# Two halves of one kernel, sliding-window attention and an SSM convolution, put into one schedule with shared memory phases

## The chip, the cores and the metric

The kernel runs on one core of a Trainium2 chip. The metric is the device time of one execution in microseconds (us). Every kernel was run with the kernel before beside it on the same chip, and medians are quoted. Names used below: PE is the matmul engine, PEld its weight load, DVE the vector engine, ACT the scalar engine, POOL the fourth compute engine, SP the engine whose queue issues most DMAs. A "kgen end" is the moment at which ACT begins to write the last part of one chunk's convolution kernel; that write takes another 0.4 us, or 1.6 us in the old form.

## The reference, cut to what matters

The output is the concatenation of two independent results, each 2048 x 640.

```python
def _A_ref(x, wqkv, wo):                       # attention: 32 heads of 20, window of 8 keys, 2 apart
    qkv = (x @ wqkv) ...                       # q, k, v: [1, 32, 2048, 20]
    idx = pos[:, None] - off[None, :]          # off = 0, 2, ..., 14
    logits = einsum("bhsd,bhswd->bhsw", q, k[idx]) * scale      # masked where idx < 0
    o = einsum("bhsw,bhswd->bhsd", softmax(logits), v[idx])
    return o @ wo

def _B_ref(u, A, B, C, log_dt, Dskip):         # SSM: a causal convolution of length 2048 per channel
    K = einsum("dn,dnl,dn->dl", Cc, exp(dt * A * l), dt * Bc).real      # 640 channels, 192 states
    y = irfft(rfft(pad(u)) * rfft(pad(K)))     # the FFT is done by matmuls in the kernel
    return y + u * Dskip
return concatenate([a, b], axis=-1)
```

There is no data that goes from one half to the other. What they share is the engines, SBUF (the on-chip buffer), the eight PSUM banks (where matmuls accumulate) and the DMA queues.

## The kernel before

The SSM half runs first, then attention, each with all eight PSUM banks and its own buffers. The SSM works on five chunks of 128 channels:

```python
for c in range(NCH):                       # NCH = 5; partB, with cuts
    X, Y = tables(tc, pools, c, Gd)        # DVE: powers of the states, from generators in DRAM (Gd)
    f1(..., U ..., A1, 0)                  # PE + ACT: first FFT stage of the input
    kgen(tc, pools, X, Y, Kd)              # PE: 512 small matmuls read X and Y; ACT evicts into Kd
    ...                                    # last chunk: load HB, the inverse FFT's table
    spread(tc, pools, C, Kd, K)            # PE + ACT
    f1(..., K ..., A1, 1)
    f2_prod(tc, pools, C, A1, Yf)          # PE + ACT + DVE: second stage and the product
    ia(tc, pools, C, Yf, Z)                # PE + ACT: first inverse stage
    nc.sync.dma_start(out=Zd[c][:], in_=Z[:])
...
Zall <- Zd                                 # DMA back, on two queues
for q in range(4):                         # inverse: 128 matmuls ps_ib, casts into ysb, DVE adds, store
    ...
```

X and Y have one buffer each, so `tables(c+1)` can't start before `kgen(c)` has read them. The generators are made in eleven rounds over all five chunks at once, ahead of the loop. The eviction in kgen writes with a stride:

```python
    for nt in (11, 11, 10):
        ps = pools["psum"].tile([128, nt, NB], f32, name="ps_k", tag="bank")     # eight banks
        ...
        nc.scalar.copy(out=Kd[:, :, t0:t0 + nt].rearrange("p b t -> p t b"), in_=ps[:])
```

Attention then does its projections, the products q*k on DVE ("prod") summed by matmuls, a softmax with maximum and sum on DVE, the products attn*v on DVE, summed by matmuls with the identity, and an output projection that contracts 32 rows at a time:

```python
    for d in range(DH):                    # 20 x 4 x 2 matmuls for 128 positions of each quarter, K = 32
        for sc in range(4):
            for eh in range(2):
                MM(pst[sc][eh][:], lhsT=o2[32*sc:32*sc+32, d, 128*q:128*q+128],
                   rhs=wo2[32*sc:32*sc+32, d, 320*eh:320*eh+320], ..., tile_position=(32*sc, 0))
```

## Time and profile before

| | kernel before |
|---|---|
| time | 666.22 us, median of 3 (662.37 to 669.65) |
| span of the profiled run | 664.6 us |
| SSM half | 0 to about 445 us |
| attention half | about 445 to 664.6 us |

The page of the profiled run gives each engine's busy time with its share of the span, and the busy tenths of 40 equal slices (16.6 us each):

```profile
PE 379.7 (57%) x6301; PEld 282.3 (42%) x6308; DVE 397.4 (60%) x578; ACT 261.1 (39%) x427; POOL 41.9 (6%) x43
...
PE   3400004775375457636761676415989944989895
...
DVE  1789647289539935991799205123009689876830
```

No engine is full over the span, but each slice has a different one that is nearly so: DVE in the prologue and in waves in the loop, PE in the projections (slices 29 to 32), DVE again in attention's products. From slice 23 to slice 30, the tail of the SSM and the start of attention, DVE does little.

The view of windows cuts the span by stage. Columns: stretch, length, then busy us (and count) of PE, PEld, DVE, ACT and POOL, then the granted PE clock, the DMA engines' mean busy share, and GB/s. The cuts are the ends of kgen(2) and kgen(4), and the end of the SSM.

```profile
0.00:251.50 251.50, 101.49 (x2368) 87.77 (x2369) 165.05 (x298) 102.51 (x139) 32.32 (x28) 0.86 0.33 89
251.50:382.80 131.30, 73.97 (x1704) 65.79 (x1705) 93.44 (x184) 56.86 (x95) 8.68 (x6) 0.71 0.11 33
382.80:445.00 62.20, 33.66 (x436) 30.48 (x435) 15.14 (x28) 31.31 (x61) 0.41 (x2) 0.77 0.59 205
445.00:664.60 219.60, 170.61 (x1793) 98.29 (x1800) 123.77 (x68) 70.45 (x133) 0.50 (x7) 0.86 0.20 54
```

Two periods of the chunk loop take 131.3 us, of which DVE works 93.4. The rest, about 19 us a period, is mostly the hole in which kgen reads the tables. DVE's timeline shows that hole (start, length, what ran; in brackets the idle time ahead of it and what ended it):

```profile
318.10 0.26 DVE L218 TENSOR_TENSOR Xtab<-Xtab,Xg 128x192 bf16<-128x192 bf16 x1 [15.80 <-DMA Xtab<-Gdram]
```

Groups of instructions that the change touches (total busy us, mean ns of one, then the engine's idle time ahead of them):

```profile
L516 DVE TENSOR_TENSOR prod<-qT,kT 128x5120 bf16<-128x5120 bf16 x16 | 44.2, 2820 | 35.9 <-ACT qT L494 33.8
L284 ACT CAST Kd<-ps_k 128x363 bf16<-128x363 f32 (+1 forms) x15 | 25.6, 1706 | 98.8 <-PE ps_k L282 98.8
...
L564 PE MATMUL ps_op<-wo_6012,o_6142 32*128 32x320 bf16 x640 | 42.9, 337 | 1.8 <-ACT ob L569 1.7
```

And one wait, of the inverse FFT on Z's way through DRAM (total us, times, longest):

```profile
PE ps_ib L427 <- DMA Zall<-Zdram_69: 9.6, 1, 9.6
```

### The profile page before, as it was taken

Reading aid. Unit: us, or ns where it says so; the run is one execution under the profiler, and the core shown is the slowest. Engines: PE = TensorE matmul, PEld = TensorE weight load, DVE = VectorE, ACT = ScalarE, POOL = GpSimd, SP = SyncE. Lnnn points to the kernel's source line nnn. Section 1 sums busy time; section 2 is a strip of 40 time slices with the busy share of each in tenths; the row PEclk is TensorE's granted clock in tenths of the full one; section 3 lists DMA queues with packets and bytes.
Section 4 is the critical chain, followed back from the end, with each engine's and each line's share of the span. In section 5 each row is a group of like instructions: output and inputs, shape, how many; then the busy total and the mean of one; then the engine's idle time right before and its main releaser. Section 6 shows DMA issues by size and latency. Waiting matters only on the chain. (4 is left out here: it accounts for less than half of the span.)

```text
span 664.6 us, 14150 instructions
## 1 busy us (share of the span) xinstructions
PE 379.7 (57%) x6301; PEld 282.3 (42%) x6308; DVE 397.4 (60%) x578; ACT 261.1 (39%) x427; POOL 41.9 (6%) x43
## 2 busy tenths in 40 slices
PE   3400004775375457636761676415989944989895
PEld 2200004665365446536551566414437622337355
DVE  1789647289539935991799205123009689876830
ACT  2865003375137524452553257333544431122222
POOL 2331200200020002000200000000000000000000
PEclk9999999986569757775876678667999975887997
DMA  3057992201110111011201093379700000001101
GB/s 91 31 152 234 262 230 54 44 1 65 37 44 1 65 38 43 1 64 39 43 1 64 3 369 140 139 162 317 175 0 3 5 0 1 0 1 41 40 15 66
DMA packets 44492, 51.27 MB, mean 77 GB/s; under 512 B 26384, under 2 KB 40976, under 8 KB 42256
## 3 DMA queue, kind: packets, MB, share of 16 engines
q1 hardware_dynamic: 33216, 33.48, 16.6%
q10 hardware_dynamic: 10512, 14.27, 7.4%
q0 software_dynamic: 704, 2.62, 2.0%
q8 instruction: 49, 0.80, 0.5%
q14 instruction: 11, 0.09, 0.0%
HBM read 33.44 MB, written 16.88 MB: 76 GB/s over the span
## 5 line engine op out<-in xcount | busy, mean ns | idle before, releaser
L277 PE MATMUL ps_k<-Ytab,Xtab 128*32 128x33 bf16 x1280 | 32.3, 278 | 67.8 <-DVE Xtab L220 35.5
L516 DVE TENSOR_TENSOR prod<-qT,kT 128x5120 bf16<-128x5120 bf16 x16 | 44.2, 2820 | 35.9 <-ACT qT L494 33.8
L284 ACT CAST Kd<-ps_k 128x363 bf16<-128x363 f32 (+1 forms) x15 | 25.6, 1706 | 98.8 <-PE ps_k L282 98.8
L218 DVE TENSOR_TENSOR Xtab<-Xtab,Xg 128x384 bf16<-128x384 bf16 (+2 forms) x35 | 14.8, 422 | 77.3 <-DMA Xtab<-Gdram 62.4
L277 PEld LDWEIGHTS <-Xtab 128*32 128x32 bf16 x1280 | 29.2, 184 | 70.6 <-issue 65.8
L357 PE MATMUL ps_ia<-cEA,Yf 128*32 128x256 bf16 x640 | 33.7, 395 | 27.3 <-DVE Yf L341 22.7
L314 PE MATMUL ps_f_521<-cBD_426,Uall 128*64 128x256 bf16 x4 | 0.7, 448 | 80.6 <-DVE Xtab L220 80.6
L314 PEld LDWEIGHTS <-Uall 128*64 128x64 bf16 x160 | 11.1, 205 | 81.6 <-issue 81.4
L564 PE MATMUL ps_op<-wo_6012,o_6142 32*128 32x320 bf16 x640 | 42.9, 337 | 1.8 <-ACT ob L569 1.7
L357 PEld LDWEIGHTS <-Yf 128*32 128x32 bf16 x640 | 30.3, 182 | 30.2 <-DVE Yf L341 23.6
L303 PE MATMUL ps_s<-Kd,cSEL 128*128 128x256 bf16 (+1 forms) x260 | 34.5, 307 | 8.4 <-ACT Kd L284 8.4
L564 PEld LDWEIGHTS <-o_6142 32*128 32x128 bf16 x640 | 31.3, 101 | 15.9 <-issue 12.7
L358 ACT CAST Z<-ps_ia 128x512 bf16<-128x512 f32 x40 | 23.7, 645 | 31.3 <-PE ps_ia L357 30.5
L237 POOL MEMSET Xtab<- 128x4608 bf16 x5 | 19.7, 3937 | 230.9 <-PE ps_k L282 230.6
L303 PEld LDWEIGHTS <-cSEL 128*128 128x128 bf16 x260 | 27.5, 115 | 14.7 <-issue 8.3
L339 DVE TENSOR_TENSOR Yf<-S 128x512 bf16<-128x512 bf16 x20 | 8.4, 420 | 34.5 <-ACT S L335 34.5
L519 PE MATMUL ps_l<-prod,Gs 128*32 128x256 bf16 x320 | 15.9, 343 | 21.8 <-DVE prod L516 21.8
L552 PEld LDWEIGHTS <-ident 128*128 128x128 bf16 x160 | 15.0, 102 | 30.6 <-issue 16.4
L282 PE MATMUL ps_k<-Ytab,Xtab 64*32 64x33 bf16 x1280 | 24.9, 239 | 5.3 <-issue 5.3
L555 ACT CAST o_6142<-ps_o 128x512 bf16<-128x512 f32 x20 | 10.2, 606 | 43.5 <-PE ps_o L552 43.5
L282 PEld LDWEIGHTS <-Xtab 64*32 64x32 bf16 x1280 | 21.6, 149 | 7.7 <-issue 6.4
L199 ACT ACTIVATE cs<-ph 128x1920 bf16<-128x1920 int32 x11 | 19.7, 1801 | 9.5 <-DVE ph L197 9.4
(725 smaller groups left out, 1010.8 us busy)
## 6 DMA issues: line engine op xcount, KB each, us to landing
Gdram<-cs SPq DMA_DIRECT2D x12, 480.0 KB, 3.1
HB<-k_HB SPq DMA_DIRECT2D x4, 1024.0 KB, 11.3
cT<-k_T ACTq DMA_DIRECT2D x1, 3072.0 KB, 24.1
Ytab<-Gdram SPq DMA_DIRECT2D x30, 96.0 KB, 2.7
Xg<-Gdram SPq DMA_DIRECT2D x5, 576.0 KB, 3.9
Uall<-in_B_u_dram POOLq DMA_DIRECT2D x4, 640.0 KB, 28.5
cSEL<-k_SEL ACTq DMA_DIRECT2D x1, 1664.0 KB, 9.7
wsb<-in_A_wqkv_dram SPq DMA_DIRECT2D x2, 800.0 KB, 21.9
```

The lines of the kernel that those rows point to most:

```text
L199: nc.scalar.activation(out=cst[:].rearrange("p c r n -> p r c n"), in_=ph[:].rearrange("p r (c n) -> p r c n", c=NCH), func=ACT.Sin, scale ...
L237: nc.gpsimd.memset(X[:, :, 20:NXS, :], 0.0)
L277: MM(o, lhsT=X[:, part, :, col], rhs=Y[:, part, :, col], start=(i == 0 and part == 0), stop=False, tile_position=(0, 32 * g), skip_group_c ...
L282: MM(o, lhsT=X[hb:hb + 64, part - 2, :, col], rhs=Y[hb:hb + 64, part - 2, :, col], start=False, stop=(part == 3), tile_position=(hb, 32 * ...
L284: nc.scalar.copy(out=Kd[:, :, t0:t0 + nt].rearrange("p b t -> p t b"), in_=ps[:])
L303: nc.tensor.matmul(o, lhsT=C["SEL"][:, wi, :], rhs=r, start=(j2 == 0 and n_ == 0), stop=(n_ == len(ops) - 1), skip_group_check=True)
L357: MM(o, lhsT=Yf[:, :, r, 4 * j + g], rhs=C["EA"][:, r, :], start=(jj == 0 and r == 0), stop=(r == 1), skip_group_check=True, tile_position ...
L358: nc.scalar.copy(out=Z[:, :, :, 4 * jq:4 * jq + 4].rearrange("p l r (j d) -> p (l r) j d", d=2), in_=ps[:].rearrange("p j l r d -> p (l r) ...
L516: V.tensor_tensor(out=pr[:], in0=q4[:, :, :, 256 * hf:256 * hf + 256], in1=k4[:, :, :, 256 * hf:256 * hf + 256], op=A.mult)
L519: MM(lps[w // 2][32 * sc:32 * sc + 32, w % 2, :], lhsT=Gs[:, ct, :], rhs=pr[:, ct, sc, :], start=(ct == 0 and w % 2 == 0), stop=(ct == 4), ...
L552: MM(ops[b][:].rearrange("p a b -> p (a b)"), lhsT=ident[:], rhs=p2[:, 2 * b:2 * b + 2, :].rearrange("p a b -> p (a b)"), start=(w == 0), ...
L564: MM(pst[sc][eh][:], lhsT=o2[32 * sc:32 * sc + 32, d, 128 * q:128 * q + 128], rhs=wo2[32 * sc:32 * sc + 32, d, 320 * eh:320 * eh + 320], s ...
```

## The change

The intent is to use one half's idle engines for the other half. The halves become one schedule. Projections, logits and softmax go under the SSM's prologue, attn*v goes into the chunk loop, and the output projection goes behind the inverse FFT with K=128, after a DMA that gathers heads across partitions. For that, memory is shared: buffers of one phase take the place of another's, and the eight PSUM banks are split by role (tags "l" 2, "a" 2, "b" 3, "k" 1). Work is cut on the way: no maximum in the softmax, its sum by matmuls, no zero slots in X, contiguous writes of Kd. The instruction order on each engine is set by a scheduler from the program's dependences, so the place of a call in the text is only a priority.

```diff
     for nt in (11, 11, 10):
-        ps = pools["psum"].tile([128, nt, NB], f32, name="ps_k", tag="bank")
+        ps = pools["psum"].tile([128, nt, NB], f32, name="ps_k", tag="k", bufs=1)
         ...
-        nc.scalar.copy(out=Kd[:, :, t0:t0 + nt].rearrange("p b t -> p t b"), in_=ps[:])
+        nc.scalar.copy(out=Kd[:, :, t0:t0 + nt], in_=ps[:].rearrange("p t b -> p b t"))
 ... (main)
-    partB(tc, pools, prm, B_u, B_Dskip, out_b)
-    partA(tc, pools, A_x, A_wqkv, A_wo, out_a, ident)
+    gens(tc, pools, ta, wi, Gd, 0, 1)          # generators of chunk 0 alone
+    make(0)                                    # tables(0), kgen(0)
+    a.transpose()
+    a.proj_qk(0)
+    a.logits(0)
+    gens(tc, pools, ta, wi, Gd, 1, 3)
+    a.proj_qk(1)
+    a.proj_v()
+    a.logits(1)
+    gens(tc, pools, ta, wi, Gd, 3, 5)
+    ... (release prologue buffers, load SEL and T)
+    avs = [(hf, dp) for hf in (1, 0) for dp in range(10)]
+    for c in range(NCH):
+        f1(U); spread; f1(K); f2_prod; ia      # arguments cut
+        nc.sync.dma_start(out=Zd[c][:], in_=Z[:])
+        if c + 1 < NCH:
+            make(c + 1)
+        ... (c == 3: release the tables, load HB in their place)
+        for hf, dp in avs[4 * c:4 * c + 4]:
+            a.av(hf, dp)
+    fp.release()                               # the FFT's buffers
+    ... Zall <- Zd, 5 DMAs, all on SP's queue
+    a.out_load()
+    a.gather(1)                                # 16 DMAs v2 -> oT
+    ... (inverse, as before, stores on SP's queue)
+    a.out_proj(1)
+    a.gather(0)
+    a.out_proj(0)
+    def av(self, hf, dp):                      # one of 20: two of the 20 head dimensions, 256 positions, 8 keys
+        p2 = self.pools["p2"].tile([128, W, 2, 256], bf16, name="p2", tag="p2")      # one buffer
+        V.tensor_tensor(out=p2[:], in0=windows(self.v2...), in1=self.at[hf]..., op=A.mult)
+        ps = self.psp.tile([128, 2, 256], f32, name="ps_o", tag="l", bufs=2)
+        for w in range(W):
+            nc.tensor.matmul(ps[:], lhsT=self.ident[:], rhs=p2[:, w], start=(w == 0), stop=(w == W - 1))
+        nc.scalar.copy(out=self.v2[:, d, HALO + 256 * hf:...], in_=ps[:])
+    def out_proj(self, hf):
+        ... 5 matmuls K=128 for each [128, 320], 160 in all, instead of 640 with K=32
```

## The prediction

> **What bounds the kernel now.** Two halves in series: in the table of windows SSM ends near 445 us, attention takes the last 220. No engine is full (page: PE 57%, DVE 60%, ACT 39%).
>
> - Prologue: in 20-66 us DVE is busy 40 of 46 us, PE 3.5.
> - Chunk loop: four periods of about 66.5 us (133-397), DVE 47-49, PE 38, ACT 30. In the timeline DVE builds tables(c+1) and f2's products in about 47 us, then idles 16 (301.9 to 318.1) while kgen reads the single table buffer.
> - SSM tail: spread, f1, f2, ia of the last chunk 383-415, Z to DRAM and back 9 us, inverse 424-445.
> - Attention: 15 us of x loading, 40 of projections, then DVE products and softmax (36.6 of 40 us in 525-565), output projection on PE.
>
> **What the change does.**
>
> DVE loses both max/sum reductions (14.8 us), subtract (4.6), half of x^T's casts (6.6): from 397 to about 370. Products keep their elements (44 each for logits and attn*v). Gens split into 1+2+2 chunks: 33 shorter rounds instead of 11, about +5 us on DVE and ACT, with one ph buffer.
>
> PE: the output projection goes from 640 K=32 matmuls (53 ns apart in the chain, 34 us) to 160 K=128, about 22 us (estimate: 320 columns at 216 ns per 512, the projections' pace).
>
> ACT: Kd's eviction now writes contiguously; it takes 1.7 us for 363 elements where other casts take 0.6 for 512: -15 us. Added: all x^T casts and about eight table loads of 1.28 us (Exp/Sin alternate). The Trainium skill, "ScalarE activation tables: per-element evaluation and per-set limits", section "What a function is on this engine", gives the same 1283 ns.
>
> Moved: projections, logits, softmax go under the prologue, tables(0) and tables(1); attn*v goes into the loop; 4 MB of Zall loads move from under the last chunk to behind it, as they reuse FFT buffers and follow Z(4) on one queue.
>
> **Sum, by DVE order** (build listing, trace durations):
> - Prologue: products 43, tables 66, gens 37, the rest 19 = 165 us, plus start and waits for projections: gens end near 200.
> - SEL and T load (11 and 26 us in before), f2(0) waits: loop proper from about 236.
> - Periods now carry attn*v: about 71, 79, 69 us to kgen(4)'s end, near 458. DVE stays the limit; kgen's wait of 15 us is only partly filled (two attn*v of 2.2 us), and kgen's single PSUM bank adds 2.
> - Tail: chain 31 us, Zall 18 (5 MB at about 300 GB/s; was 9), inverse 21, rest of output projection 20, gather and last store 5.
>
> Predicted **552 us**, range 512 to 598. Faster by over 2%: 0.96; within 2%: 0.03; slower: 0.01.
>
> **What would show it.** PE busy with attention in the first 200 us; DVE total 365-375 us, over 65% of the span; first loop chunk held by cT's DMA; DVE idle 10-14 us at kgen(2), (3), (4); PE idle 15-20 us before the inverse, ended by Zall's DMA; Kd casts below 0.8 us; output projection near 22 us of PE, after the inverse.
>
> **What would make it wrong.** In-order engines: a product ahead of table work holds DVE until ACT has evacuated q and k; two PSUM banks per role may starve PE. PE's clock (0.68-0.75 granted in the loop) may fall as PE gets denser. Gens' stores may block behind x loads on the SP queue. The other way: attn*v fills kgen's wait: 510.

## The result, and the profile after

| | before | after |
|---|---|---|
| median (range), 4 runs each on one chip | 667.17 us (662.37 to 669.65) | 584.19 us (583.37 to 585.86) |
| span of the profiled run | 664.6 us | 581.5 us |
| granted PE clock over the span | 0.821 | 0.839 |

The ratio is 0.8767, with a 95% interval of 0.8713 to 0.8822. A ratio is the mean time of one kernel's fast runs over that of the other's of the same rounds, so it isn't quite the ratio of the medians quoted. The change is worth 83 us, and 32 us less than predicted.

The page after, same lines (slices of 14.5 us):

```profile
PE 389.3 (67%) x5764; PEld 278.0 (48%) x5784; DVE 371.4 (64%) x646; ACT 268.1 (46%) x510; POOL 45.3 (8%) x60
...
PE   2769934899864159979659967579843397417467
...
DVE  0548999459999961799991699871999504102200
```

From slice 4 to slice 31 DVE is now mostly at 8 or 9 tenths. The exceptions are slices 8 and 9, the change from the prologue to the loop (slice 16) and kgen's holes (slices 22 and 28). Behind kgen(4), in the last 109 us, it has little to do. The windows, cut again at the ends of kgen(2) and kgen(4):

```profile
0.00:319.30 319.30, 224.58 (x3388) 154.66 (x3398) 242.24 (x424) 167.60 (x313) 44.43 (x56) 0.87 0.29 85
319.30:472.10 152.80, 100.33 (x1781) 73.75 (x1791) 114.08 (x194) 55.96 (x105) 0.91 (x4) 0.79 0.10 32
472.10:581.50 109.40, 64.36 (x596) 49.63 (x596) 15.07 (x28) 44.52 (x93) 0.00 (x0) 0.81 0.56 176
```

Length less DVE's busy time is DVE's idle time. This one column accounts for the result:

| DVE busy / idle, us | before | after |
|---|---|---|
| SSM to the end of kgen(4) (after: with attention in it) | 258.5 / 124.3 | 356.3 / 115.8 |
| tail (SSM; after: with the output projection) | 15.1 / 47.1 | 15.1 / 94.3 |
| attention by itself | 123.8 / 95.8 | none |
| sum | 397.4 / 267.2 | 371.4 / 210.1 |

So 83 us = 26 us less work on DVE + 57 us less idle time. The idle time that went is attention's own, 95.8 us. The SSM's body lost only 8.5 us of its 124 us of idle time, although attention was laid over it, and the tail's rose by 47.2 us. So the SSM's holes are hardly smaller than before. Attention's DVE work stands mostly end to end with the SSM's, and the projections, evictions and loads behind it run meanwhile. The table can't tell whether the new order made holes of its own, which attention then filled; e3_ssm below shows that it did, to some 19 us.

DVE's timeline at kgen's hole, where before it stood 15.80 us in one piece:

```profile
315.82 2.29 DVE L477 TENSOR_TENSOR p_5850<-v_1847,attn 128x4096 bf16<-128x4096 bf16 x1 [10.04 <-PE ps_o L481]
324.06 0.26 DVE L221 TENSOR_TENSOR Xtab<-Xtab 128x192 bf16<-128x192 bf16 x1 [5.95 <-DMA Xtab<-Gdram]
...
404.31 0.26 DVE L221 TENSOR_TENSOR Xtab<-Xtab 128x192 bf16<-128x192 bf16 x1 [11.34 <-DMA Xtab<-Gdram]
```

The first line is an attn*v product that waits 10 us for the identity matmuls to read the only p2 buffer: PE is in kgen. Then the reload of the tables takes 6 us more. Together it is 16 us again; the hole is as long as before, with one product of 2.3 us moved into its middle.

The groups:

```profile
L456 DVE TENSOR_TENSOR prod<-q,k 128x2048 bf16<-128x2048 bf16 x40 | 48.3, 1237 | 6.7 <-ACT q L432 4.0
...
L288 ACT CAST Kd<-ps_k 128x363 bf16<-128x363 f32 (+1 forms) x15 | 6.8, 453 | 64.7 <-PE ps_k L286 64.7
...
L509 PE MATMUL ps_op<-wo,oT 128*128 128x320 bf16 x160 | 26.8, 331 | 14.1 <-ACT ob L510 8.2
```

Kd's casts fell from 1706 to 453 ns, the output projection from 42.9 to 26.8 us. The wait on Zall doubled, for its loads now follow the last chunk's FFT:

```profile
PE ps_ib L657 <- DMA Zall<-Zdram_62: 18.6, 1, 18.6
```

In the tail SP's queue and PE look like this (SPq is the time in which a queue issues; x16 is sixteen DMAs):

```profile
513.54 17.10 SPq L497 DMA_DIRECT2D oT<-v_1847  x16
531.07 15.80 SPq L662 DMA_DIRECT2D out_dram<-ysb  x16
546.92 1.57 SPq L512 DMA_DIRECT2D out_dram<-ob  x2
```

```profile
550.60 9.45 PE L509 MATMUL ps_op<-wo,oT 128*128 128x320 bf16 x50 [8.24 <-ACT ob L510]
564.82 13.23 PE L509 MATMUL ps_op<-wo,oT 128*128 128x320 bf16 x80 [4.77 <-DMA oT<-v_1847]
```

The first output rows of attention, cast at 531 us, leave at 547 us, behind sixteen stores of the SSM; with two buffers ob, PE then waits 8.24 us. The second half of the gather is issued behind those and costs 4.77 us.

### The profile page after: what moved, and what is told of

Its sections match the earlier page's. It is cut to its first block, busy times and chain, and to the rows that moved or that the text cites. A ratio compares the mean times of both kernels' runs of the same rounds, so it can differ in the third digit from the quotient of the medians.

```text
span 581.5 us, 13349 instructions
## 1 busy us (share of the span) xinstructions
PE 389.3 (67%) x5764; PEld 278.0 (48%) x5784; DVE 371.4 (64%) x646; ACT 268.1 (46%) x510; POOL 45.3 (8%) x60
## 4 chain that ended last, share of the span: by engine, by line
DVE 46%; PE 26%; DMA 11%; ACT 8%; issue 6%; SPq 3%; ACTq 0%; POOL 0%; DVEq 0%
PE ps_k L281 5%; DVE Xtab L222 4%; DVE Xtab L225 4%; DVE prod L456 4%; PE ps_k L286 4%; PE ps_o L481 4%; PE ps_op L509 3%; DMA wo<-in_A_wo_dram 2%; DVE Ytab L224 2%; DVE Ytab L223 2%; PE ps_s L307 2%; ACT S L339 2%; DVE Ytab L221 2%; DMA Ytab<-Gdram 2%; DVE Ytab L226 2%
## 5 line engine op out<-in xcount | busy, mean ns | idle before, releaser
L456 DVE TENSOR_TENSOR prod<-q,k 128x2048 bf16<-128x2048 bf16 x40 | 48.3, 1237 | 6.7 <-ACT q L432 4.0
L208 POOL TENSOR_SCALAR mc<-wi 128x384 int32<-128x384 int32 (+1 forms) x33 | 37.6, 1142 | 112.8 <-DVE ph L209 94.5
L361 PEld LDWEIGHTS <-Yf 128*32 128x32 bf16 x640 | 25.9, 181 | 24.1 <-DVE Yf L345 13.2
L459 PE MATMUL ps_l<-prod,cGs 128*32 128x512 bf16 x160 | 20.2, 497 | 25.4 <-DVE prod L456 25.4
L288 ACT CAST Kd<-ps_k 128x363 bf16<-128x363 f32 (+1 forms) x15 | 6.8, 453 | 64.7 <-PE ps_k L286 64.7
L211 ACT ACTIVATE cs<-ph 128x768 bf16<-128x768 int32 (+1 forms) x33 | 24.4, 738 | 25.9 <-DVE ph L210 17.8
L509 PE MATMUL ps_op<-wo,oT 128*128 128x320 bf16 x160 | 26.8, 331 | 14.1 <-ACT ob L510 8.2
L426 PE MATMUL ps_k<-xT,w_301 128*128 128x270 bf16 x200 | 29.8, 294 | 4.3 <-ACT q L432 2.2
L509 PEld LDWEIGHTS <-oT 128*128 128x128 bf16 x160 | 17.0, 107 | 23.6 <-issue 15.3
L441 PE MATMUL ps_v<-xT,w_305 128*32 128x512 bf16 x400 | 24.1, 384 | 5.0 <-ACT v_1847 L443 5.0
L657 PE MATMUL ps_ib<-Zall,HB 128*128 128x160 bf16 x128 | 12.8, 269 | 21.5 <-DMA Zall<-Zdram_62 18.6
L426 PEld LDWEIGHTS <-w_301 128*128 128x128 bf16 x200 | 19.7, 102 | 14.2 <-issue 7.1
## 6 DMA issues: line engine op xcount, KB each, us to landing
cT<-k_T SPq DMA_DIRECT2D x1, 3072.0 KB, 13.8
```

The source lines that it names most:

```text
L208: nc.gpsimd.tensor_scalar(out=mc, in0=wi[:, s], scalar1=float(2.0 ** (29 - k)), scalar2=None, op0=A.add)
L211: nc.scalar.activation(out=cs.rearrange("p c r n -> p r c n"), in_=ph.rearrange("p r (c n) -> p r c n", c=n), func=ACT.Sin, scale=PHS)
L361: MM(o, lhsT=Yf[:, :, r, 4 * j + g], rhs=C["EA"][:, r, :], start=(jj == 0 and r == 0), stop=(r == 1), skip_group_check=True, tile_position ...
L426: MM(ps[:], lhsT=self.wk[:, kt, cs], rhs=self.xT[:, kt, p0:p0 + HALO + 256], start=(kt == 0), stop=(kt == 4))
L441: nc.tensor.matmul(ps[32 * sc:32 * sc + 32, :], lhsT=self.wv[:, kt, d:D:DH], rhs=self.xT[:, kt, HALO + 512 * sc:HALO + 512 * sc + 512], st ...
L456: V.tensor_tensor(out=pr[:], in0=self.q[:, ct].unsqueeze(1).to_broadcast([128, 2, 4, 256]), in1=windows(self.k[:, ct, :, 12 - 4 * m:12 - 4 ...
```

## The experiments

The theory after the result had three parts. (1) The gain is the overlap of attention's idle time, not the removed work. (2) The loop is additive in DVE's time, as one p2 buffer keeps attn*v out of kgen's hole. (3) The tail is too long by waits on DMA order and on Zall. The rivals are given with each run. Medians of different batches, which ran on different chips, are compared directly; the kernel before had medians of 665.04, 662.04, 666.16 and 664.35 us in the four batches, so a difference of a few us between batches is not safe by its median alone. Where the ratios tell something else, this is said.

### e1_tailq: the tail's DMAs on two queues

```diff
-        nc.sync.dma_start(out=Zall[:, c], in_=Zd[c][:])
+        (nc.sync if c % 2 == 0 else nc.scalar).dma_start(out=Zall[:, c], in_=Zd[c][:])
 ... and likewise for wo, the gathers to oT, the stores of ysb and ob
```

> The changed kernel with one edit: the DMAs of the tail (Zall, wo, oT gathers, ysb and ob stores) alternate between the SP and ACT queues, as the kernel before has them, instead of all on SP. In the changed kernel SP issues 16 gathers in 17.1 us and 16 ysb stores in 15.8 us one behind the other, and the first ob store waits behind them until 546.9. Theory (the one queue orders and paces the tail): 584 falls to 568 to 575, and the time from kgen(4)'s end to the end of the span falls from 109 us to about 95. Rival (the tail is paced by the DMA engines themselves, 320-byte and 512-byte packets, share 0.77 in 521 to 550): the time stays within 4 us of 584.

Measured: 580.21 us (579.48 to 580.46), ratio 0.8738. The gain is 4 us by the medians, and the ratio's interval (0.8688 to 0.8788) overlaps that of after (0.8713 to 0.8822), so even this isn't sure. The theory's total fell, and so did its tail of 95 us (107 measured); the rival's "within 4 us" held. ACT's list of waits has one behind the gathers on its own queue:

```profile
ACT ysb L659 <- DMA oT<-v: 24.0, 1, 24.0
```

The Trainium skill, "DMA: Bandwidth & Descriptors", section "Issuing engines are not separate DMA queues", says that DMAs from several engines run on the same 16 DMA engines, and that issuing from more of them only saves time on the sequencer. The small gain agrees. The 24.0 us are not the price of the gathers, though: for most of that time no cast was ready, as PE waited 21.5 us for Zall and began the inverse at 523.6 us. In after the first cast began 1.0 us behind the first of these matmuls, here 3.2 us (526.8). So the eight gathers that ACT issued ahead of it held ACT's casts for about 2 us (an estimate from these two distances).

### e2_zall: Zall loaded early

Zall takes the place of the tables (free after kgen(4)), chunks 0 to 3 are loaded there under the last chunk, and ia(4) writes its part in place, not through DRAM. HB takes the FFT's place.

```diff
+            Zall = ip.tile([128, NCH, 64, 2, 32], bf16, name="Zall")     # ip: where the tables were
+            for cz in range(NCH - 1):
+                nc.sync.dma_start(out=Zall[:, cz], in_=Zd[cz][:])
 ...
-        ia(tc, pools, C, Yf, Z)
-        nc.sync.dma_start(out=Zd[c][:], in_=Z[:])
+        ia(tc, pools, C, Yf, Zall[:, c])       # last chunk only
```

> The changed kernel with Zall placed where the tables were, so that its chunks 0 to 3 load under chunk 4 and ia(4) writes its part in place without the trip through DRAM; the HB constants take Zall's old place and load after f2(4). Theory (PE's 18.6 us of waiting for Zall before the inverse is exposed time): about 15 us less, 567 to 572, and PE's wait before the inverse falls below 5 us. Rival (HB's 4 MB or the later stores take the place of the wait, since the DMA engines are what is full): 578 to 584.

Measured: 569.31 us (567.15 to 570.75), ratio 0.8578: 15 us, as the theory had it. PE's wait ahead of the inverse fell from 18.6 to 0.77 us. The waits behind the inverse stayed: 8.4 us of PE for ob and 12.2 us, in two waits, for oT.

### e3_ssm: after, without attention

All calls of attention are taken out. The output's attention half isn't written, so the result is wrong.

> The changed kernel without any attention work (its half of the output is left unwritten, so the result is wrong on purpose). It measures what the SSM half alone takes in the new schedule. Theory (a large part of the SSM half's own path became shorter, because chunk 0's gens are made alone and the loop lost the table memset): about 395 us, so attention costs about 190 us in the new schedule against 220 in the old one, and less than half of the 83 us gained is overlap. Rival (the gain is overlap, the SSM path is as long as before): about 440 us, attention costs 145.

Measured: 469.18 us (two runs). Both theories fell: the SSM by itself takes longer in the new schedule than it took in the old one, where it ended near 445 us. Its windows, cut at its own kgen ends:

```profile
0.00:260.90 260.90, 106.68 (x2368) 88.97 (x2369) 165.06 (x370) 102.93 (x184) 58.75 (x47) 0.79 0.29 84
260.90:392.50 131.60, 79.89 (x1704) 67.73 (x1704) 92.60 (x184) 49.62 (x95) 0.97 (x4) 0.73 0.12 37
392.50:467.50 75.00, 39.17 (x436) 34.63 (x435) 15.02 (x28) 31.09 (x61) 0.00 (x0) 0.75 0.51 176
```

Against before, the prologue with the first chunks is 9 us longer at the same DVE work (165.06 and 165.05 us), the loop is the same (131.6 and 131.3 us), and the tail is 13 us longer, of which Zall's wait is 8.4 us (18.0 against 9.6). So the new order costs the SSM 22 us, and attention on top of it costs 584.2 - 469.2 = 115 us, where it took 220 us. It brings 371.4 - 272.7 = 99 us of DVE work with it. That the two are near each other is chance, as the stretches of after against this run show: to the end of kgen(2) 58.4 us more for 77.2 us of DVE work, in the two periods 21.2 us more for 21.5 us, and in the tail 34.4 us more for none. So 19 us of attention's DVE work went into holes of the SSM, all of it ahead of the end of kgen(2); in the two periods it adds in full, which is part (2); and the tail pays for the output projection, the gather and the stores.

### e4_work: before, with two pieces of the removed work

```diff
-        nc.scalar.copy(out=Kd[:, :, t0:t0 + nt].rearrange("p b t -> p t b"), in_=ps[:])
+        nc.scalar.copy(out=Kd[:, :, t0:t0 + nt], in_=ps[:].rearrange("p t b -> p b t"))
 ... and the softmax of after: Exp straight from PSUM, no maximum, the sum by 8 identity matmuls (ps_n)
```

> The kernel before with only two of the removed pieces of work and no new schedule: the softmax without the maximum and with its sum on PE, and Kd's eviction written contiguously. Theory (removed work is the smaller part of the gain): 10 to 14 us from the serial softmax, 6 to 9 us from five Kd evictions in the chain, so about 645 us. Rival (removed work is most of the gain): 610 or less.

Measured: 653.76 us (653.15 to 654.95), ratio 0.985 (0.9793 to 0.9907): 11 us. The rival fell, and the theory's 16 to 23 us were too much as well. The verdict at 2% is unclear, but it bounds the share of these two pieces in the 83 us: less than a fifth in the serial kernel. The rest of the removed work wasn't tried there, above all the output projection with K=128 (16 us less of PE's time) and the casts that went from DVE to ACT.

### e5_p2x2: two buffers for the attn*v product

```diff
-        p2 = ...tile([128, W, 2, 256], bf16, name="p2", tag="p2")
+        p2 = ...tile([128, W, 2, 256], bf16, name="p2", tag="p2", bufs=2)
```

> After with two buffers for the attention product p2 instead of one. In after the vector engine stood 10.0, 6.0, 3.9 and 12.1 us before an attn*v product, waiting for the identity matmuls ps_o to read the only p2 buffer, while PE was in kgen. Theory (the single buffer keeps attn*v out of kgen's gap): these waits shrink to under 10 us in all, one more product of 2.3 us fits into each kgen gap, the periods between the ends of kgen fall from 83/80/72 by 2 to 5 us each, total 570 to 578 us. Rival (the waits sit where the vector engine would next wait for kgen's table buffer and the reload anyway, so they only change name): waits move to Xtab, total within 3 us of after (581 to 587).

Measured: 575.54 us (575.12 to 577.19), ratio 0.8696: 8.6 us. The total is the theory's, but the waits it named hardly shrank, to 26.4 us in four waits (32.0 before: 12.1, 10.0, 6.0 and 3.9). At one of kgen's holes:

```profile
328.42 2.29 DVE L477 TENSOR_TENSOR p<-v,attn 128x4096 bf16<-128x4096 bf16 x1 [9.99 <-PE ps_o L481]
332.84 0.26 DVE L221 TENSOR_TENSOR Xtab<-Xtab 128x192 bf16<-128x192 bf16 x1 [2.12 <-DMA Xtab<-Gdram]
```

The products run further ahead: 17 of the 20 begin before the end of kgen(2), where it was 10 in after. That end comes 8.5 us later for it (327.8 us), and the two periods to kgen(4), with three products left instead of ten, take 135.7 us instead of 152.8. DVE's idle time is 71.0 us before the end of kgen(2) and 36.0 us in the two periods, against 77.1 and 38.7 in after; the difference, 8.8 us, is the gain. (The ratios, 0.8696 against 0.8767, make it 4.7 us, with intervals that just overlap: this batch ran on another chip. It is the idle times of the traces that show the gain.) At this hole the pieces are 9.99, 2.12, 0.69 and 0.42 us, 13.2 in all, against 10.04, 5.95 and 1.20 us, 17.2 in all. So part (2) holds in that the buffer mattered, but it is wrong that the buffer alone keeps attn*v out: with two, the next product still waits for PE, which is in kgen, and most of the hole is left.

### e7_kdold: the old eviction of Kd

```diff
-        nc.scalar.copy(out=Kd[:, :, t0:t0 + nt], in_=ps[:].rearrange("p t b -> p b t"))
+        nc.scalar.copy(out=Kd[:, :, t0:t0 + nt].rearrange("p b t -> p t b"), in_=ps[:])
```

> After with the old order of Kd's eviction (strided write), so ACT's casts take 1.7 us again instead of 0.45. With one PSUM bank for kgen, its three parts wait for the eviction. Theory: two of the three casts per chunk lie in the chain (bank k has one buffer), 2.5 us per chunk, so 8 to 13 us slower than after (592 to 597). Rival (PE and ACT have slack there, as the run with the removed work alone gained only 11 us from three changes together): under 4 us, 584 to 588.

Measured: 597.25 us (595.70 to 598.63), ratio 0.9019: 13 us slower than after, the theory's upper end. kgen(4) ends at 485.9 instead of 472.1 us. The wait of kgen's next part for the eviction, in this run and then in after:

```profile
PE ps_k L281 <- ACT Kd L288: 12.3, 9, 2.6
```

```profile
PE ps_k L281 <- ACT Kd L288: 2.5, 3, 1.4
```

That is 9.8 us of the 13; the spread's matmuls wait 2.9 us for Kd instead of 0.5. In the serial kernel, with eight banks, the spread's wait was the only one on the eviction that its list shows (8.4 us in five), and the same edit together with the cheaper softmax gave 11 us (e4). With one bank for kgen the eviction's length is part of the chain. The split of PSUM by role had a price of its own, and the contiguous write paid for it.

### e6_k32: the output projection as before, without the gather

```diff
-        self.wo_sb = op.tile([128, 5, D], bf16, name="wo")            # and the 32 gathers v2 -> oT
+        self.wo_sb = op.tile([128, DH, D], bf16, name="wo2")          # wo four times, 3.3 MB
 ...
+                        nc.tensor.matmul(pst[sc][:], lhsT=self.v2[32 * sc:32 * sc + 32, d, ...], rhs=self.wo_sb[32 * sc:32 * sc + 32, d, ...], ..., tile_position=(32 * sc, 0))
```

> After with the output projection as before it: 640 matmuls with K=32 straight from v2, no gather to oT, and wo loaded four times (3.3 MB) in the tail. Theory (full K pays): PE's busy time for ps_op rises from 26.8 to about 43 us at the end, with nothing to hide it; 5 to 15 us slower than after. Rival (the gathers' DMA, 17 us of the SP queue for half of it, costs what full K saves): the wait of the stores behind the gathers goes, and the time is within 5 us of after, or below.

Measured: 612.58 us (612.37 to 613.39), ratio 0.925: 28 us slower, beyond both.

```profile
L503 PE MATMUL ps_op<-wo,v 32*128 32x320 bf16 x640 | 57.3, 362 | 12.2 <-ACT ob L506 12.2
```

PE's time for the projection rose by 30.5 us, from 26.8 to 57.3 us, about as much as the total. The gather is worth its DMAs. (The edit also gives ob four buffers and the projection two more PSUM banks.) That it is 57.3 and not the 42.9 us of the kernel before comes from the first half: its matmuls followed each other in 157 to 168 ns (64 in 10.06 us), those of the second half in 48 ns (80 in 3.86 us). The windows of these two groups, with the granted clock as the third number from the end:

```profile
547.19:557.25 10.06, 10.06 (x64) 6.55 (x64) 0.00 (x0) 0.28 (x1) 0.00 (x0) 0.50 0.01 2
589.71:593.57 3.86, 3.86 (x80) 2.70 (x80) 0.00 (x0) 0.98 (x4) 0.00 (x0) 1.00 0.48 170
```

The first group had half the clock, 0.50 against 1.00. That is a factor of two of the 3.3; the rest is left open. So the 28 us are not the price of K=32 alone.

### e8_avend: attn*v kept out of the loop

The scheduler moves products forward (17 of 20 ahead of kgen(2)'s end in e5_p2x2), so moving the call was not expected to be enough, and was not tried. A copy of one element makes each product depend on the last chunk's Kd:

```diff
+            V.tensor_copy(out=p2[:, 0, 0, 0:1], in_=Kds[NCH - 1][:, 0, 0:1])     # overwritten by the product
 ...
-        for hf, dp in avs[4 * c:4 * c + 4]:
+        for hf, dp in (avs if c + 1 == NCH else []):
```

> After with all 20 attn*v products kept out of the chunk loop: a one-element copy makes each depend on the last chunk's Kd, so they run under and behind the last chunk's chain (about 40 small copies more). In after, the two periods between the ends of kgen(2) and kgen(4) took 152.8 us with 114.1 us of the vector engine busy; the run without attention 131.6 with 92.6. Theory (attn*v in the loop is additive, the loop hides nothing of it): these two periods fall to 130 to 134 us, kgen(4) ends 40 to 48 us earlier (424 to 432), the tail grows by the part of 46 us of products that doesn't fit the 28.7 us hole before the last f2, plus gather and output projection behind it; total 575 to 595 us. Rival (the loop does hide attn*v under PE and ACT work): kgen(4) ends less than 20 us earlier and the total is 605 us or more.

Measured: 645.60 us (643.22 to 649.08), ratio 0.9722: 61 us slower than after, the rival's total. Yet the loop did what the theory said. Its two periods, then the stretch that follows:

```profile
303.50:433.70 130.20, 80.85 (x1711) 68.41 (x1714) 95.01 (x186) 50.87 (x97) 0.92 (x4) 0.74 0.12 38
433.70:562.00 128.30, 77.83 (x458) 37.25 (x463) 55.24 (x62) 30.90 (x56) 0.00 (x0) 0.75 0.05 20
```

kgen(4) ends at 433.7 us, 38.4 us earlier than in after. So 20 products cost the loop 1.9 us each, no more than DVE's time for one, 2.3 us. Behind the loop they cost 6 us each:

```profile
498.93 2.29 DVE L479 TENSOR_TENSOR p<-v,attn 128x4096 bf16<-128x4096 bf16 x1
501.28 3.10 PE L483 MATMUL ps_o<-p,cident 128*128 128x512 bf16 x8 [2.58 <-DVE p L479]
...
504.61 2.29 DVE L479 TENSOR_TENSOR p<-v,attn 128x4096 bf16<-128x4096 bf16 x1
506.96 3.59 PE L483 MATMUL ps_o<-p,cident 128*128 128x512 bf16 x8 [2.58 <-DVE p L479]
```

With one buffer DVE and PE take turns: 2.3 us of product, then 3.1 to 3.6 us of matmuls, start to start 5.7 to 6.2 us. In the loop the matmuls' part lies under other DVE work; alone it doesn't. So both were half right. The loop adds most of a product's DVE time (1.9 of 2.3 us), and hides everything else of it. What was wrong is the sum of 46 us for the products at the end: it counted one engine of a pair that alternates.

The matmuls ran at half pace here. The Trainium skill, "TensorE: Matmul & The Clock Gate", section "Wait — 56ns, not 53.3ns?", gives a start-to-start of 426.7 ns for 512 columns on the cold clock and 215.7 on the warm one. The trace agrees: in the groups of 3.59 us six of the seven steps from start to start are 426 or 427 ns, and the granted clock between 494 and 520 us was 0.57; in the loop of after eight of them at 300 us start 215 or 216 ns apart.

### b4_early, b5_late10, b5_late5, b6_poolq: a version that beats both

b4_early takes e2 and e5 together, and loads wo and one half of the gather into the place of the tables, and puts the first half of the output projection ahead of the inverse; ob gets four buffers.

```diff
+        if c + 2 == NCH:
+            pools["op"] = ip                   # where the tables were
+            a.out_load()
+            a.gather(1)
 ...
+    a.gather(0)
+    a.out_proj(1)                              # ahead of the inverse
     for q in range(4):
         ysb = ...
```

> Meant to beat both: Zall early in the tables' place and the inverse table in the FFT's (as in e2), two p2 buffers (as in e5), and half of the gather and wo loaded inside the loop, so that half of the output projection runs before the inverse and its stores don't queue behind the SSM's. The e2 and e5 gains add: 584.2 - 15 - 9 = 560. Theory (the tail is paced by DMA, 15 us for one half of the gather, 16 for the SSM stores): another 12 to 20 us, 540 to 549. Rival (only the exchange of waits, as with the alternating queues): 555 to 561.

Measured: 552.39 us (551.62 to 554.14), ratio 0.8318. The two gains add to 560.7, so the rest brought 8 us, between the theory's 12 to 20 and the rival's nothing. The tables' place is free only at 467.7 us, after kgen(4), so wo and the first gather weren't early at all, and the second one held the stores behind it:

```profile
494.81 20.44 SPq L497 DMA_DIRECT2D oT<-v  x16
515.35 2.03 SPq L512 DMA_DIRECT2D out_dram<-ob  x4
```

The next two hold back 10 or 5 of the 20 products, as in e8, to the 28 us that DVE waits ahead of the last f2.

> b4_early with the second ten attn*v products held back to the last chunk's Kd by a one-element copy each. If attn*v is additive in the loop and there is a hole of 28 us on the vector engine before the last f2: kgen(4) ends 15 to 20 us earlier, the chain after it grows by 5 to 10, the gather and the second half of the output projection come later; 530 to 542 us. Rival (identity matmuls and evacuations stand in the last chain's way, and the gather waits for them): equal to b4_early or slower.

> b4_early with only the last five attn*v products held back (4, 4, 4, 3 in the loop). Theory: half of the gain of b5_late10 in the loop, without its growth of the tail; 532 to 545 us. Rival as there: equal to b4_early.

Measured: 559.77 us (558.68 to 561.25) with ten, 556.06 us (553.59 to 559.37) with five. kgen(4) ended at 453.0 and 458.9 us instead of 467.7, so the loop did get shorter by 14.7 and 8.8 us, but what follows it grew from 84.7 to 106.0 and 92.9 us. The rival held: DVE's hole before the last f2 is one in which PE and ACT do the last chunk's chain, and the gather waits for the products (with ten held back it began at 489.9 us instead of 474.9). An idle DVE was not spare time.

In b6_poolq the 32 gathers of b4_early go to POOL's queue, which has nothing else to do by then.

```diff
-                nc.sync.dma_start(out=self.oT[hf]..., in_=self.v2...)
+                nc.gpsimd.dma_start(out=self.oT[hf]..., in_=self.v2...)
```

> b4_early with the 32 gathers of both halves issued from POOL's queue instead of SP's. In b4_early the second half's gather held SP's queue for 20.4 us (494.8 to 515.4), and ACT waited 7.6 and 7.5 us before output casts for the stores behind it. Theory (order on one queue holds the stores): these two waits fall to under 2 us each, the first output store leaves before 505 us, 538 to 548 us in all. Rival (the 16 DMA engines are the limit in this stretch, as for the alternating queues in e1, which gave 4 us): 549 to 555 us, the waits only change name. [...] if each of its issues takes over 1.5 us, slower than b4_early.

Measured: 545.91 us (545.36 to 547.49), ratio 0.822 (0.8177 to 0.8263): 6.5 us less than b4_early, and correct. The first stores of ob now leave at 498.5 us instead of 515.4:

```profile
498.46 4.41 SPq L512 DMA_DIRECT2D out_dram<-ob  x4
```

One of ACT's two waits for the stores went, the other stayed (7.5 us): it is behind the SSM's fourteen stores, 14.3 us of the same queue. So the order on one queue is a part of the tail that bandwidth doesn't explain. This is the fastest version here, 38 us under after and 118 us under the 664.35 us of before in its batch.

## Why the prediction was right or wrong

It was right in direction and within its range of 512 to 598, and 32 us too low. Some 28 us of these are in the two sums below; the rest is mostly that the sums are of the span, which was 2.7 us shorter than the median time.

**What held.**

- DVE's total: 365 to 375 predicted, 371.4 measured. The estimate of the removed and added DVE work was right.
- The mechanism, "by DVE order": the body is DVE's work put end to end. By 214 us, the end of the generators, DVE had done 166.9 us of work (165 predicted).
- PE busy with attention in the first 200 us: between 98 and 154 us it was busy 50.5 us of 56, most of it with attention (kgen(0)'s matmuls take 11.5 us of that time and overlap with others).
- The wait for Zall: 18 predicted, 18.6 measured, and e2 showed that it is worth 15 us of the total. The last chunk's chain (31 predicted, from kgen(4)'s end to Z's store at 503.7 us) and the inverse (21 predicted, 521.5 to 542.4 us) were also right.
- Kd's casts below 0.8 us: 0.45. They count, but not for the reason given ("-15 us" of ACT): e7 showed 13 us, since with one bank PE waits for them. The text had only "kgen's single PSUM bank adds 2".
- PE's clock was not lower for the denser work: 0.839 against 0.821.

**What failed, term by term.** The sum was 458 us to the end of kgen(4) and 95 us for the tail.

- "Gens end near 200": 213.6 us. DVE's work was as predicted, so the 14 us are idle time of the prologue. Its causes weren't tested one by one.
- "First loop chunk held by cT's DMA; loop proper from about 236": products of the first f2 began at 239.6 us, but T had landed earlier (issued at 216.5, 13.8 us to landing). kgen(1), spread and f1 lay in between on PE. So the number was right by luck: the generators ended 14 us late, and the stretch behind them took 26 us instead of 36.
- "Periods ... about 71, 79, 69 us": from 236 us to the ends of the next kgens it was 83, 80 and 72. The step that failed is "kgen's wait of 15 us is only partly filled (two attn*v of 2.2 us)", and with it "DVE idle 10-14 us". The holes were no shorter in idle time, 16 us at kgen(2) (10.04 and 5.95) and 15 at kgen(3) (3.92 and 11.34). A product waits for a p2 buffer, which waits for PE, which is in kgen; a second buffer gave 8.6 us (e5), and left most of the hole. In the three periods together DVE idled 51 us, where three times 10 to 14 were predicted. That it is the first period which is 12 us too long has another reason: products ran ahead, eight of them lie in it, and DVE works 70.7 of its 83 us. kgen(4) ended at 472 instead of 458 us.
- "Rest of output projection 20, gather and last store 5": 39 us from the inverse's end at 542.4 us to 581.5. PE took 26.8 us for the projection, not 22, and waited 8.2 us for stores and 4.8 us for the gather. The estimate gave the gather no place in the queue, and no wait to the stores. Its pace of the matmuls was right at the full clock, where they start 136 ns apart; but right behind the wait of 8.24 us the granted clock was half (0.50, then 1.00), and 18 of them took as long as the next 34:

```profile
550.60:555.20 4.60, 4.60 (x18) 2.56 (x18) 0.00 (x0) 1.49 (x4) 0.00 (x0) 0.50 0.49 135
555.20:560.05 4.85, 4.79 (x34) 3.06 (x32) 0.00 (x0) 2.63 (x7) 0.00 (x0) 1.00 0.46 127
```

  This is the other 14 us; b6_poolq and e2 together with e5 show that they, and Zall's wait, can be had back.
- "Over 65% of the span": 64%, for the span was longer.
- "About eight table loads" more: there are 14 in after and 3 in before. Each takes 1283 ns, as the trace shows and the Trainium skill says in "ScalarE activation tables: per-element evaluation and per-set limits", section "What a function is on this engine".

**Where the gain came from, which the prediction didn't say.** Attention costs 115 us where it cost 220 (e3), and the new order takes 22 us back from the SSM. Two pieces of the removed work are 11 us in the serial kernel (e4). The cheaper output projection is 16 us of PE's time that wasn't tried there, so some 56 to 72 us are left for overlap. The overlap is only in part of the kind intended, where one half's holes are filled by the other's work (19 of attention's 99 us on DVE): elsewhere DVE's work adds, and what is hidden is what attention needs from other engines and DMA.

**What stays open.** The prologue's 14 us; how much the cheaper output projection alone is worth; and why the matmuls of e6's first half, at half the clock, ran at a third of the second half's pace. No run separates what the halved clock costs in the tail.

## What to carry to other kernels

When two halves are laid over each other, count for each stretch the work of the engine that limits both: its work adds, and only its idle time can vanish. So the sum of its work is a floor (371.4 us of DVE here), and the waits of the half that is moved are the first to go (95.8 us here). A hole in that engine's work is only filled by what doesn't need the engine that made the hole; here each product waited for a buffer that PE had to empty, while PE was what everybody waited for. And what leaves the middle of a kernel gathers in its tail, where here the order of DMAs on one queue cost 6.5 us (b6_poolq): start loads where the space is free first, and don't issue anything that waits ahead of a store that is ready.

## What the Trainium skill lacked or had wrong

- "ScalarE: Activation LUTs", section "What ACT_TABLE_LOAD costs", gives 186 ns + 0.833 ns per element for an ACTIVATE with immediate operands; an estimate by that formula is 488 ns for 363 elements. Kd's eviction of 363 elements with a contiguous write took 461 ns on the mean, near it; the same cast with a strided write took 1765 ns before and 1742 ns in e7_kdold. The section doesn't speak of the output's stride; "SBUF — State Buffer" speaks of strides in general, but has no time for a write of ACT.
- "DMA: Bandwidth & Descriptors", section "Issuing engines are not separate DMA queues", says that more issuing engines only save time on the sequencer, and that this time is usually small. Here it wasn't small: sixteen gathers held SP's queue for 20.4 us (b4_early; the trace doesn't tell issuing from waiting for room), and moving the gathers to POOL's queue gave 6.5 us (b6_poolq), as ready stores no longer stood behind them.
- "TensorE: Matmul & The Clock Gate", section "HAM oscillation — how this bites in real kernels", states the rule as no idle gaps of PE over about 3.4 us. In e8_avend the gaps were 2.58 to 2.65 us by the profile, in rounds of 6 us, and the granted clock was 0.57 with matmuls 427 ns apart. Gaps below that length were not safe here. The page's next section does tell of short idle times between groups of matmuls that make the clock swing, but gives no length for them.
